# Batch 0's first q and last v in head pairs, W1's second quarter in halves, and a new order of the opening

## The chip, the cores and the metric

The kernel runs on one core of one Trainium2 chip. The metric is the device time of one execution in microseconds. Before the change the median of three runs was 257.46 us (256.84 to 258.04).

The core has five engines with queues of their own, each worked through in order: TensorE (PE, with its weight loads shown as PEld), VectorE (DVE), ScalarE (ACT), GpSimd (POOL) and SyncE (SP, which here only issues DMAs). An instruction that waits holds up all that stands behind it on its engine. Tiles lie in SBUF; matmuls write to PSUM, which has eight banks.

## What is computed

Linear attention on 8 batches, 8 heads, 576 positions and 64 columns a head, and a two-layer network over all 4608 tokens:

```python
q_s = softmax(q, axis=-1)          # over the 64 columns of a head
k_s = softmax(k, axis=2)           # over the 576 positions
kv  = einsum('bhsd,bhse->bhde', k_s, v)
x   = einsum('bhsd,bhde->bhse', q_s, kv)   # -> (4608, 512)
h   = x @ w_in                     # 512 x 2048
out = (h * sigmoid(h)) @ w_out     # 2048 x 512
```

Inputs and output are float32.

## The kernel before

The tokens are done in tiles: tile 0 is the whole of batch 0 (576 tokens), then come tiles of 448 and 512 tokens. The attention of a later batch is computed beside the network of an earlier tile. From tile 1 on the network's products are done by a scheme with seven products in place of eight, for which sums and differences of weights (`WS`, `T1` to `T4`) are made once by VectorE.

All instructions are issued from one list of names, `ORDER` (line 18), written out by hand: the order of the names gives the order on each engine and each DMA queue. Only dependencies between tiles set waits beyond it. `op` (line 584) binds each name to a function.

The names that matter for the opening, with `b.c` standing for batch and half of the heads (c = 0 is heads 0 to 3, c = 1 is heads 4 to 7; a half consists of two head pairs):

- `lq`, `lk`, `lv` load a half of q, k or v (`load`, line 146; 576 KB). Batch 0's go through SP's queue, those of batches 1 and 2 through POOL's, later ones through SP's again.
- `eq` is exp of q on ScalarE (line 160), `z` the row sums and reciprocal on VectorE (line 203), `n` the product with it (line 213). `tr` transposes q on TensorE in nine pieces (line 231) and `tc..a`, `tc..b` copy the result out of PSUM, five pieces on ScalarE and four on VectorE (line 240).
- `ek` is exp of k on ScalarE (line 167). `vc` casts v into `vaug` (line 170), which has a column of constants beside each head for the sums over positions.
- `kv` (line 244) multiplies k and v, 36 small matmuls for a half, row block by row block (nine of them); `kc` (line 256) divides by the sums, giving `kvn`.
- `X` multiplies q with `kvn` (line 278) and `x..a`, `x..v` copy the token tile out to `XT` (line 288).
- `heat0` to `heat3` are matmuls on a constant tile whose results nobody reads (line 561).
- `W1a0`, `W1a1`, `W1b`, `W1c`, `W1d` load w_in in four quarters of four blocks of 128 columns (line 565), with a cast to float16 on the way, through POOL's queue. W1a is in two halves of rows already. The name `gate` stands ahead of them: a copy of one element of k0.0 on GpSimd, so that W1's transfers start when that k has landed. `W2a` to `W2d` load w_out (line 571). The transfers of q1, k1 and v1 stand between these in the same queue.
- The wide stage: for each of the 16 blocks fb, `w{fb}.0` and `w{fb}.1` are four matmuls each of 288 columns (line 304, matmul at 307), over rows 0 to 255 and 256 to 511 of w_in; `h{fb}` is a tanh on ScalarE (line 318), `v{fb}` a product on VectorE (line 322). `WIDE` (line 302) gives the PSUM banks, in turn 4, 2, 0 and 6, so w(fb+4) waits for v(fb). `p{fb}` (line 443) is the second layer of the first 512 tokens.
- `WS{g}.{i}` (line 372) are VectorE's sums and differences of w_in: `WS1.1` needs W1b, `WS1.3` W1b and W1d, `WS0.3` W1a and W1c.

Batch 1's attention (`eq1`, `qp1`, `z1`, `n1`, `ek1`, `vc1`, `tr1`, `tc1`, `kv1`, `kc1`, `xt1`, `x1`) is laid between the end of the wide stage and the `p` steps.

Four very small reads, `touch` (line 547), stand at the start of GpSimd's queue; they fetch a few elements of w_in, w_out, k and v of batch 0 into a tile that is overwritten later.

Of the kernel before, what the change touches and what calls it, by code (L numbers as in the profile page):

```python
# [8 lines left out]
FP32 = mybir.dt.float32  # L9
# [12 lines left out]
    w5.0 w5.1 v0 v2 h3 w4.0 w4.1 WS0.1 h5 w6.0 w6.1 v3 h4 W2b2 v4 w7.0 w7.1 v5 w8.0 w8.1 h7 h6 v7 w9.0 w9.1 lv1.0 h8  # L22
    v6 w11.0 w11.1 v8 h9 lv1.1 w10.0 w10.1 eq1.0.0 v9 h11 WS0.2 w12.0 w12.1 eq1.1.0 v11 h10 w13.0 w13.1 WS1.1
    eq1.0.1 v10 h12 w15.0 w15.1 qp1a h13 v12 w14.0 w14.1 eq1.1.1 v13 qp1b WS1.2 W2c1 p0 h14 z1.0 ek1.0 p1 z1.1.0
    n1.0 z1.1.1 p2 h15 ek1.1 v15 p3 WS1.4 W2c2 tr1.0 v14 lq2.0 p4 tc1.0a tc1.0b lq2.1 n1.1 p5 W2d p6 lk2.0 T1 vc1.0
    lk2.1 p7 tr1.1 lv2.0 vc1.1a vc1.1b gcopy WS1.3 kv1 lv2.1 tc1.1b p8 tc1.1a kc1 WS0.3 xt1.0 xt1.1 x1.0a x1.1v p9
    x1.2a x1.3v g1.1.1 xs1.1 xs1.2 xs1.4 g1.1.2 s1.1.0a WS0.4 p10 xs1.3 eq2.0 a1.1.0 p11 eq2.1 z2.0 g1.1.6 g1.1.5
    s1.1.1a z2.1 n2.0 p12 ek2.0 g1.1.7 p13 s1.1.2v n2.1 ek2.1 p14 a1.1.2 g1.1.4 p15 tq2 u1.1.4 g1.1.3 po2v vc2.1
    po1a m0 po3v po0a a1.1.1 u1.1.0 vc2.0 m1 lk3.0 mu0 m2 T2 lq3.0 mu1 lq3.1 m3 u1.1.2 lk3.1 T3 m4 lv3.0 u1.1.1
    lv3.1 m5 T4 mu2 os0 mu4 kv2 mu5 m6 mu3 kc2 X2.0 mu6 X2.1 x2.0v m7 x2.1a x2.3a x2.2v g2.1.1 mu7 xs2.1 xs2.2  # L30
    g2.1.2 s2.1.0v b1.1.0 ek3.0 S1.1 g2.1.6 eq3.1 lk4.0 S1.2 b1.2.0 os1 s2.1.1a b1.1.1 xs2.3 xs2.4 eq3.0 a2.1.0
    g2.1.7 vc3.0 sa1 b1.2.1 lq4.0 z3.1 s2.1.2a g2.1.5 vc3.1 ek3.1 b1.6.0 a2.1.2 n3.1 lk4.1 g2.1.4 z3.0 g2.1.3 u2.1.0
    g2.0.2 u2.1.4 wa1 n3.0 b1.6.1 a2.1.1 u2.1.2 g2.0.1 sb1 S1.3 kv3 tq3 s2.0.0a b1.5.0 kc3 u2.1.1 S1.4 g2.0.6 b1.7.0
    s2.0.1v lv4.0 ek4.1 b1.7.1 lv4.1 a2.0.0 os3 g2.0.7 sc1 ek4.0 b1.5.1 s2.0.2v g2.0.5 eq4.0 lk5.0 wc1 lq4.1 g2.0.4
    a2.0.2 os2 b1.4.0 vc4.0 lk5.1 z4.0 u2.0.4 g2.0.3 u2.0.2 b1.3.0 lv5.0 vc4.1 a2.0.1 u2.0.0 lq5.0 b1.4.1 n4.0 X3.0
    wl1v X3.1 kv4 x3.0a x3.1v x3.2a b1.3.1 kc4 x3.3a xs3.1 u2.0.1 g3.1.1 xs3.2 wb1 g3.1.2 s3.1.0a xs3.3 xs3.4 g3.0.2
    S2.1 g3.1.6 S2.2 eq4.1 b2.2.0 s3.1.1a b2.1.0 z4.1 ek5.0 b2.1.1 a3.1.0 g3.1.7 n4.1 sa2 ek5.1 b2.6.0 s3.1.2v
    g3.1.5 vc5.0 tq4 g3.1.4 a3.1.2 u3.1.0 b2.6.1 u3.1.4 S2.3 g3.1.3 sb2 lq5.1 g3.0.1 u3.1.2 a3.1.1 lv5.1 lk6.0
# [24 lines left out]
    s8.0.2v b7.7.1 a8.0.2 b7.5.1 sc7 u8.0.0 g8.0.4 wc7 g8.0.3 u8.0.4 b7.4.0 a8.0.1 u8.0.2 b7.3.0 u8.0.1 b7.3.1 e1.0
    wb7 S8.1b e1.1 o7.0 S8.1a b7.4.1 S8.2a sa8 S8.2b e2.0 wl7v e6.0 S8.3 o7.1 e6.1 e2.1 sb8 e5.0 waE0 S8.4 qa00g
    qa01s e7.0 waE1 e7.1 qa11g qa10a e5.1 sc8 wcE0 e3.0 wcE1 qc01g wxE0 qc11a e3.1 wbE0 qc00a wxE1 qb00g qb01s e4.0
    wbE1 qc10s qb10g e4.1 qb11s wlE0a ql01a ql00s wlE1a ql11a ql10s
"""


@with_exitstack  # L70
def kernel(
# [9 lines left out]
    nc = tc.nc  # L81
    B, H, S, D = q.shape
# [737 lines left out]
```

## Time and profile before

| what | value |
|---|---|
| median of three runs | 257.46 us (256.84 to 258.04) |
| the profiled execution, whole time | 257.18 us |
| its span in the trace | 255.1 us |
| granted TensorE clock, mean | 0.999 |
| DMA rate over the span, mean | 180 GB/s |
| first matmul of the wide stage (line 307) starts | 15.07 us |
| first matmul of the second layer (line 445) starts | 30.76 us |

Landings of the opening's transfers (start of the issue plus time to landing, from the DMA issues of the trace), in us:

| transfer | issued | landed |
|---|---|---|
| q0.0, q0.1 (SP) | 0.74, 1.27 | 4.34, 6.04 |
| k0.0, v0.0 (SP) | 1.76, 2.27 | 8.39, 9.82 |
| k0.1, v0.1 (SP) | 2.79, 3.33 | 11.32, 12.78 |
| W1a0, W1a1 (POOL) | 8.59, 9.34 | 14.22, 15.51 |
| W1b, W1c, W1d (POOL) | 10.08, 10.83, 11.56 | 18.51, 20.96, 23.57 |
| q1.0, q1.1 (POOL) | 12.29, 13.00 | 25.04, 26.50 |
| W2a (POOL) | 13.73 | 28.93 |
| k1.0, k1.1 (POOL) | 14.80, 16.05 | 30.43, 31.90 |
| W2b1, W2b2 (POOL) | 18.80, 21.25 | 33.00, 34.30 |
| v1.0, v1.1 (POOL) | 23.86, 25.69 | 35.83, 37.29 |

A row of a timeline gives the start, the length, the engine, the line, the operation, what is written and read, and the shape; in brackets stands the idle time of the engine before it and what ended it. SPq and POOL rows named DMA_DIRECT2D are the issues of transfers, not the transfers. Rows with xN are N instructions in a row put together. The chain of waits is followed back from the last instruction of the kernel to what released each one. An engine's busy share is over the whole span.

### The profile page before, as it was taken

The page shows a single profiled execution, that of the slowest core. Times are in us where ns is not written, and L with a number is a line of the kernel's source. Part 1 is how long each engine was busy: PE and PEld are TensorE (multiplying, and loading weights), DVE is VectorE, ACT ScalarE, POOL GpSimd, SP SyncE. Part 2 cuts the span into 40 slices and gives each one's busy share as a digit, 9 for nine tenths or more (in the row PEclk, how much of TensorE's full clock was granted, in tenths as well). Part 3 has the DMA queues.
Part 4 walks back from the last instruction along what each step waited for, and adds up shares of the span by engine and source line. Part 5 has one row for each costly group of instructions (what it writes and reads, how often), then busy time and mean ns, then how long its engine had stood idle before and what let it go on. Part 6 is the DMA issues. An engine that isn't in the chain of part 4 may idle for free.

```text
span 255.1 us, 6464 instructions
## 1 busy us (share of the span) xinstructions
PE 248.8 (98%) x2732; PEld 204.5 (80%) x2732; DVE 205.6 (81%) x276; ACT 190.9 (75%) x225; POOL 67.6 (27%) x66
## 2 busy tenths in 40 slices
PE   8799999999999999999999999999999999999994
PEld 3467746757888888888888888888888888888883
DVE  2958999987999989998998986896569836886752
ACT  4766886898999999999879979737587656664311
POOL 4652592630541531430083050006000000000022
PEclk9999999999999999999999999999999999999999
DMA  6999999879969938996965950030807000700355
GB/s 239 350 197 299 300 301 310 340 175 395 356 119 279 403 114 216 345 296 155 299 241 87 251 195 0 3 67 18 174 4 164 4 0 4 155 12 0 69 139 123
DMA packets 36172, 45.89 MB, mean 180 GB/s; under 512 B 16416, under 2 KB 21216, under 8 KB 36144
## 3 DMA queue, kind: packets, MB, share of 16 engines
q1 hardware_dynamic: 29456, 33.56, 45.5%
q0 software_dynamic: 6288, 11.60, 17.7%
q10 hardware_dynamic: 400, 0.33, 0.6%
q8 instruction: 21, 0.34, 0.5%
q14 instruction: 7, 0.06, 0.1%
HBM read 36.70 MB, written 9.44 MB: 181 GB/s over the span
## 4 chain that ended last, share of the span: by engine, by line
PE 91%; DMA 5%; ACT 1%; SPq 1%; DVE 0%; issue 0%; ACTq 0%
PE PS L503 37%; PE PS L425 36%; PE PS L307 6%; PE PS L445 5%; DMA vt<-in_v_dram 4%; PE PS L335 2%; PE PS L282 2%; PE PS L248 2%; SPq L152 1%; DMA out_dram<-ow 1%; PE PS L234 0%; DVE ow L754 0%; ACT ow L767 0%; ACT vaug L142 0%; ACT sc L739 0%; ACT XT L142 0%
## 5 line engine op out<-in xcount | busy, mean ns | idle before, releaser
L403 DVE TENSOR_TENSOR h<-PS,h 128x1024 f32<-128x1024 f32 (+1 forms) x45 | 54.1, 1205 | 8.9 <-PE PS L425 7.9
L503 PEld LDWEIGHTS <-GT 128*128 128x128 f16 x512 | 50.1, 98 | 5.9
L425 PEld LDWEIGHTS <-WS 128*128 128x128 f16 x480 | 46.6, 98 | 6.7 <-issue 0.8
L409 ACT ACTIVATE GT<-h 128x1024 f16<-128x1024 f32 (+1 forms) x45 | 46.8, 1049 | 1.1 <-DVE h L403 1.0
L503 PE MATMUL PS<-W,GT 128*128 128x256 f16 x384 | 47.3, 273 | 0.0
L425 PE MATMUL PS<-XS,WS 128*128 128x256 f16 (+1 forms) x360 | 45.0, 272 | 0.0
L142 ACT COPY h<-PS 128x1024 f32<-128x1024 f32 (+1 forms) x31 | 31.1, 1004 | 17.1 <-PE PS L425 16.0
L503 PEld LDWEIGHTS <-S 128*128 128x128 f16 x384 | 37.1, 98 | 4.6
L425 PEld LDWEIGHTS <-W 128*128 128x128 f16 x360 | 35.2, 98 | 4.4
L216 POOL TENSOR_TENSOR eq<-eq,rzq 128x1152 bf16<-128x1152 bf16 x13 | 27.4, 2117 | 37.5 <-DVE rzq L211 36.6
L503 PE MATMUL PS<-T,S 128*128 128x256 f16 x256 | 32.2, 273 | 0.0
L144 POOL CAST vaug<-vt 128x1152 bf16<-128x1152 f32 x12 | 15.8, 1332 | 60.5 <-DMA vt<-in_v_dram 60.1
L425 PE MATMUL PS<-XT,W 128*128 128x256 f16 (+1 forms) x240 | 29.7, 272 | 0.0
L144 DVE COPY h<-PS 128x1024 f32<-128x1024 f32 (+1 forms) x14 | 17.0, 1213 | 8.8 <-PE PS L425 3.9
L772 POOL DMA_DIRECT2D out_dram<-ow x5 | 2.7, 547 | 70.0 <-DVE ow L754 70.0
L163 ACT ACTIVATE eq<-qt 128x1152 bf16<-128x1152 f32 (+1 forms) x18 | 18.8, 1055 | 2.9 <-DMA qt<-in_q_dram 2.7
L168 ACT ACTIVATE ek<-kt 128x1152 bf16<-128x1152 f32 x16 | 18.6, 1163 | 1.7 <-DMA kt<-in_k_dram 1.5
L207 DVE TENSOR_REDUCE zq<-eq 128x18 f32<-128x1152 bf16 x14 | 18.8, 1343 | 1.3 <-ACT eq L163 1.2
L409 ACT ACTIVATE GT<-PS 128x1024 f16<-128x1024 f32 (+1 forms) x15 | 15.2, 1013 | 6.1 <-PE PS L425 6.1
L503 PE MATMUL PS<-T,GT 128*128 128x256 f16 x128 | 16.3, 273 | 0.0
L503 PE MATMUL PS<-W,S 128*128 128x256 f16 x128 | 16.1, 273 | 0.0
L307 PE MATMUL PS<-XT,W 128*128 128x288 f16 x128 | 15.9, 286 | 0.0
(89 smaller groups left out, 334.1 us busy)
## 6 DMA issues: line engine op xcount, KB each, us to landing
out_dram<-ow SPq DMA_DIRECT2D x64, 128.0 KB, 2.9
qt<-in_q_dram SPq DMA_DIRECT2D x11, 576.0 KB, 6.2
kt<-in_k_dram SPq DMA_DIRECT2D x11, 576.0 KB, 7.1
vt<-in_v_dram SPq DMA_DIRECT2D x11, 576.0 KB, 6.5
qt<-in_q_dram POOLq DMA_DIRECT2D x4, 576.0 KB, 9.9
kt<-in_k_dram POOLq DMA_DIRECT2D x4, 576.0 KB, 13.2
vt<-in_v_dram POOLq DMA_DIRECT2D x4, 576.0 KB, 11.8
W<-in_moe_w_in_dram POOLq DMA_DIRECT2D x3, 512.0 KB, 10.1
```

The lines of the kernel that those rows point to most:

```text
L142: eng.copy(out=o, in_=i)
L144: eng.tensor_copy(o, i)
L163: nc.scalar.activation(out=half(st[b]["eq"], cc)[:, :, g0:g1], in_=jgd(b, "qt", cc)[:, :, g0:g1], func=ACT.Exp)
L168: nc.scalar.activation(out=half(ek, cc), in_=jgd(b, "kt", cc), func=ACT.Exp)
L207: nc.vector.reduce_sum(out=z, in_=e, axis=AX.X)
L216: eng.tensor_tensor(out=e, in0=e, in1=r[:, :, :, None].to_broadcast([128, J, 2, D]), op=ALU.mult)
L307: nc.tensor.matmul(out=PS[:, WIDE[fb] + n, 0:S // 2], lhsT=W1[:, c, fb * 128:(fb + 1) * 128], rhs=XTS[0][:, c, n * (S // 2):(n + 1) * (S / ...
L403: nc.vector.tensor_tensor(out=four(t, i), in0=group_bank(t, g), in1=four(t, i), op=ALU.add)
L409: nc.scalar.activation(out=group_out(t, f, n), in_=x, func=ACT.Silu, scale=1.0 / XS)
L425: nc.tensor.matmul(out=PS[:, bank + p // 2, (p % 2) * HT:(p % 2) * HT + width(t)], lhsT=a[:, c, p * 128:(p + 1) * 128], rhs=bb[:, c, 0:wid ...
L445: nc.tensor.matmul(out=PS[:, 2 + tb, :], lhsT=GTS[t % 2][:, fc, tb * 128:(tb + 1) * 128], rhs=W2[:, fc, :], start=(fc == 0), stop=(fc == N ...
L503: nc.tensor.matmul(out=PS[:, bank, m * HN:(m + 1) * HN], lhsT=a[:, fc, m * 128:(m + 1) * 128], rhs=bb[:, fc, :], start=(first and fc == 0) ...
```

## The change

Batch 0's first q (`lq0.0`) and last v (`lv0.1`) are loaded in two transfers each, one for each head pair. The exp and the row sums of q0.0 are done a head pair at a time. The cast of the second head pair of the last v is split: rows 0 to 4 on VectorE (`vc0.1b`), rows 5 to 8 on ScalarE (`vc0.1c`, new). W1's second quarter, `W1b`, is loaded in two halves of rows (`W1b0`, `W1b1`).

The order is new from the first name up to batch 1's x: `tr0.0` and `tc0.0a` stand ahead of `ek0.0`, `tr0.1` ahead of `kv0.0`, `tc0.1b` ahead of `kc0.0`, `heat1` ahead of `tr0.0`, and `heat3` ahead of `X0.0`; the order of the wide stage's blocks, of batch 1's loads against W2's and of the WS steps differs. Behind `x1` the list is as before.

Batch 7's first k and v are loaded whole, as the load in two parts is kept for its first q only. The small reads go through a helper that now takes an engine; all four are given GpSimd, as before.

```diff
-    lq0.0 lq0.1 lk0.0 lv0.0 lk0.1 lv0.1 heat0 eq0.0 z0.0 eq0.1 gate W1a0 W1a1 W1b W1c W1d lq1.0 lq1.1 W2a n0.0 z0.1
-    ek0.0 tr0.0 heat1 n0.1 vc0.0 tc0.0a tc0.0b kv0.0 kc0.0 tr0.1 ek0.1 X0.0 heat2 vc0.1a vc0.1b tc0.1a tc0.1b kv0.1
-    kc0.1 heat3 x0.0a x0.0v X0.1 w0.0 x0.1a x0.1v w2.0 lk1.0 w1.0 w1.1 lk1.1 w2.1 h1 w0.1 h2 v1 w3.0 w3.1 h0 W2b1
...
+    lq0.0.0 lq0.0.1 lq0.1 lk0.0 lv0.0 lk0.1 lv0.1.0 lv0.1.1 gate W1a0 W1a1 W1b0 W1b1 W1c W1d heat0 eq0.0.0 eq0.0.1
+    eq0.1 heat1 z0.0.0 z0.0.1 n0.0 tr0.0 z0.1 tc0.0a ek0.0 n0.1 tc0.0b vc0.0 lq1.0 tr0.1 ek0.1 vc0.1a lq1.1 tc0.1b
+    W2a kv0.0 vc0.1c heat3 kc0.0 X0.0 heat2 vc0.1b tc0.1a x0.0a kv0.1 kc0.1 x0.0v X0.1 w0.0 x0.1v w2.0 w1.0 W2b1
+    x0.1a w0.1 h0 WS0.1 w1.1 v0 w3.0 w2.1 h1 v1 w3.1 w4.0 lk1.0 W2b2 w5.0 w5.1 h2 v2 lv1.0 w6.0 h3 v3 h5 w4.1 v5
+    w6.1 lk1.1 lv1.1 WS1.1 W2c1 w7.0 h4 w7.1 h6 h7 v4 w9.0 w9.1 w8.0 w8.1 v6 v7 h9 v9 w11.0 h8 w11.1 WS1.3 WS0.3
+    w10.0 v8 h11 WS1.2 w10.1 w13.0 w13.1 eq1.0.1 h10 eq1.0.0 qp1a v11 w12.0 w12.1 h13 v10 w15.0 qp1b v13 eq1.1.1 h12
...
-    def load(b, name, src, cc, eng, parts=1):
-        t = ld.tile([128, 2, J * D], FP32, name=name)
-        st[b][name, cc] = t
+    def load(b, name, src, cc, eng, g0=0, g1=2):
+        if (name, cc) not in st[b]:
+            st[b][name, cc] = ld.tile([128, 2, J * D], FP32, name=name)
+        t = st[b][name, cc]
...
+        eng.dma_start(out=t[:, g0:g1], in_=x[:, 2 * cc + g0:2 * cc + g1, :])
+
+    def loads(b, name, src, cc, eng, parts):
         for g in range(0, 2, 2 // parts):
-            h = slice(g, g + 2 // parts)
-            eng.dma_start(out=t[:, h], in_=x[:, 2 * cc:2 * cc + 2, :][:, h, :])
+            load(b, name, src, cc, eng, g, g + 2 // parts)
...
-    def vcast(b, cc, eng, g0=0, g1=2):
-        o = vaug[:, :, 2 * cc + g0:2 * cc + g1, 0:D]
-        i = jgd(b, "vt", cc)[:, :, g0:g1, :]
+    def vcast(b, cc, eng, g0=0, g1=2, j0=0, j1=J):
+        o = vaug[:, j0:j1, 2 * cc + g0:2 * cc + g1, 0:D]
+        i = jgd(b, "vt", cc)[:, j0:j1, g0:g1, :]
...
-    touch(0, w_in[0:510])
...
+    for i, x in enumerate((w_in[0:510], w_out[0:2046], k[0].rearrange("h s d -> (h s) d"), v[0].rearrange("h s d -> (h s) d"))):
+        touch(i, x, nc.gpsimd)
...
+            if (x, c) in (("q", 0), ("v", 1)):
+                for g in range(2):
+                    op(f"l{x}0.{c}.{g}", load, 0, x + "t", src, c, nc.sync, g, g + 1)
+            else:
+                op(f"l{x}0.{c}", load, 0, x + "t", src, c, nc.sync)
+        if c == 0:
+            for g in range(2):
+                op(f"eq0.0.{g}", exp_q, 0, 0, g, g + 1)
+                op(f"z0.0.{g}", qsum, 0, 0, g)
...
-    op("vc0.1b", vcast, 0, 1, nc.vector, 1, 2)
+    op("vc0.1b", vcast, 0, 1, nc.vector, 1, 2, 0, 5)
+    op("vc0.1c", vcast, 0, 1, nc.scalar, 1, 2, 5, J)
...
-("W1b", 4, 4, 0, 4), 
+("W1b0", 4, 4, 0, 2), ("W1b1", 4, 4, 2, 4), 
...
-                op(f"l{x}{b}.{c}", load, b, x + "t", src, c, dma, 2 if b == 7 and c == 0 else 1)
+                op(f"l{x}{b}.{c}", loads, b, x + "t", src, c, dma, 2 if (x, b, c) == ("q", 7, 0) else 1)
```

More of the change, by code (lines that the diff above doesn't have):

```diff
@@ L24 @@
[L24 to L38, printed above, removed]
@@ L618 @@
     op("gate", lambda: nc.gpsimd.tensor_copy(gate, st[0]["kt", 0][0:1, 1, 0:1]))
[L619 removed]
+    for x, f, n, c0, c1 in (("W1a0", 0, 4, 0, 2), ("W1a1", 0, 4, 2, 4), ("W1b0", 4, 4, 0, 2), ("W1b1", 4, 4, 2, 4), ("W1c", 8, 4, 0, 4), ("W1d", 12, 4, 0, 4)):
         op(x, load_w1, f, f + n, c0, c1)
```

87 lines of the change are left out of this document (48 added, 39 removed).

## Prediction

> **What bounds the kernel now.** I read the page's busy times first, then the chain of waits in order of time, then the timeline of the first 16 us, then the DMA issues one by one. Busy times, and the shares of the chain by engine:
>
> ```profile
> PE 248.8 (98%) x2732; PEld 204.5 (80%) x2732; DVE 205.6 (81%) x276; ACT 190.9 (75%) x225; POOL 67.6 (27%) x66
> ...
> PE 91%; DMA 5%; ACT 1%; SPq 1%; DVE 0%; issue 0%; ACTq 0%
> ```
>
> TensorE is the bound, and the 5% of DMA has to be found in time. The chain in order of time (start, length, what) has it in one piece:
>
> ```profile
> 3.33 9.45 DMA vt<-in_v_dram
> ...
> 12.81 0.67 ACT vaug L142
> 13.48 0.59 ACT qT L142
> 14.07 0.60 ACT XT L142
> ...
> 14.70 0.44 PE PS L282 x8
> 15.14 15.79 PE PS L307 x128
> 30.92 3.45 PE PS L445 x16
> ```
>
> The last of batch 0's loads (lv0.1) is issued at 3.33 and lands 9.45 later, at 12.78. Until then nothing can be done about it; from 15.07 on TensorE has work without a gap (windows of 1 us over the wide stage are busy 1.00 each, and the waits of PE after 12 us are empty) until its tail at 250 us. So the kernel's time is (start of the first wide matmul) + 240 us, unless an edit tears a hole into the rest. What lies between the landing and that start is read from the timeline (start, length, engine, line, what):
>
> ```profile
> 10.21 1.36 DVE L216 TENSOR_TENSOR eq<-eq,rzq 128x1152 bf16<-128x1152 bf16 x1
> 11.06 0.48 PE L248 MATMUL PS<-vaug,ek 64*64 64x65 bf16 x36 [0.21 <-ACT vaug L142]
> 11.49 1.17 ACT L168 ACTIVATE ek<-kt 128x1152 bf16<-128x1152 f32 x1
> 12.73 0.82 PE L563 MATMUL PS<-XS 128*128 128x512 f16 x3
> 12.81 0.67 ACT L142 CAST vaug<-vt 128x576 bf16<-128x576 f32 x1 [0.15 <-DMA vt<-in_v_dram]
> 12.81 0.76 DVE L144 CAST vaug<-vt 128x576 bf16<-128x576 f32 x1 [0.51 <-DMA vt<-in_v_dram]
> 13.53 0.56 PE L248 MATMUL PS<-vaug,ek 64*64 64x65 bf16 x36
> 14.35 0.29 DVE L261 TENSOR_TENSOR kvn<-PS,rz 128x128 bf16<-128x128 f32 x1
> 15.07 1.15 PE L307 MATMUL PS<-XT,W 128*128 128x288 f16 x8
> ```
>
> Both casts of the last v start 0.03 after the landing and take 0.67 and 0.76; kv0.1 follows at 13.53, ends at 14.09; its normalisation and X0.1 take the 0.98 up to 15.07. The window 2 to 11 us has the DMA engines busy 0.95 to 1.05, so 12.78 itself is set by bytes, and no bytes are added or taken away.
>
> **The change part by part.** Durations are from this execution (span 255.1, 257.18 with what lies around it; the median of the runs is 257.46, so 0.28 above it).
>
> *Casts of the last v.* lv0.1 comes in two head pairs. k0.1 landed at 11.32 and v0.1 at 12.78, so the first half should land about half way, at 12.05 (bounds: 11.32 and 12.78). ScalarE takes exp of k0.1 at 11.35 instead of 11.49, because tc0.0a, which stood ahead of it at 10.91, now runs before ek0.0; it ends at 12.52, and vc0.1a (0.67) runs from about 12.45 to 13.1. The other half is now shared: 5 of 9 rows on VectorE, 4 of 9 on ScalarE. ScalarE's casts of 1152 and 576 columns took 1.16 and 0.67, so 0.85 ns a column and 0.18 fixed, and 256 columns are 0.40: 13.0 to 13.4. VectorE's 320 columns lie between its 0.42 for 512 bf16 columns out of PSUM (11.48) and its 0.76 for 576 of this cast; scaled like ScalarE's they are 0.50: 12.81 to 13.31. kv0.1 goes over the rows in order, 4 products each; rows 5 to 8 come 0.28 after the first, so the late piece is no wait. It can start at 13.33 and take the 0.48 of kv0.0 (its own 0.56 had a wait for VectorE's cast in it), so it ends at 13.81 against 14.09: **0.28 won**.
>
> *The first q in halves.* This decides whether TensorE is free by then, as tr0.1 now stands ahead of kv0.0. Halves are 0.73 to 0.85 apart (576 KB land 1.46 to 1.70 apart), so the first lands near 3.6 (bounds 3.5 and 4.34). Exp halves 0.68: 3.6 to 4.3 and 4.36 to 5.04. Half sums of 0.71 (L209 took 1.35 for two): the second ends at 5.79. Reciprocal 0.27, n0.0 1.36: 7.47, against 8.61. z0.1, reciprocal and n0.1 behind it (1.35, 0.27, 1.36): 10.43 against 11.57. tr0.1 is then through at 11.0, kv0.0 runs at 11.05 (its v, cast at 9.85, was ready at 11.01 as before), kvn at 12.05, X0.0 12.1 to 12.45, heat2's three matmuls (0.22 each) to 13.1. That is before 13.33. On ScalarE tc0.0a waits for tr0.0 until 7.95 and ends at 8.65; ek0.0 behind it starts 0.13 later than before and still ends before v0.0 lands at 9.82. If the first half came no earlier than the whole did, 4.34, the same sums give n0.1 at 11.0, kv0.0 11.55, X0.0 12.65, heat2 to 13.7, kv0.1 ending at 14.2: 0.1 **lost**. Bounds of the opening: 0.45 won (VectorE's piece at 0.42, and kvn and X without their 0.1 of waits) to 0.1 lost. I take 0.26 won, 0.28 less 0.02 for the semaphore of the third cast: first wide matmul at **14.81**. ScalarE's x0.0a, which it needs, ran from 13.97 to 14.67 and keeps that place, so it is no limit yet.
>
> *Two more issues on SP* (0.49 each): the last v half is issued at 4.8, for bytes that move near 12. Nothing.
>
> *The wide stage.* 128 matmuls in 15.79 are 0.4935 for each half step w. New turns are 14.81 + 0.4935 x place. W1b's halves: lands were 14.22, 15.51 (W1a), 18.51 (W1b), 20.96, 23.57. w4.0 (place 8, 18.76) needs W1b0, about 17.0; w5.1 (place 10, 19.75) needs W1b1, 18.51: cover 1.2. Before, w5.0 had its turn at 19.02: cover 0.5. W1c is needed at 22.7, W1d by WS1.3 on VectorE at 25.5: covers 1.7 and 1.9. VectorE now does WS1.3, WS0.3 and WS1.2 (0.61 apart) ahead of v8 and v11. Laid end to end from v9 (ends 25.2): v8 to 27.1, v11 to 28.55; w12.0 (bank of w8) has its turn at 27.6, w15.0 (bank of w11) at 28.63. Cover 0.5 and 0.1; semaphore gaps of 0.03 to 0.07 can eat the second, so 0 to 0.2 of stall. I take 0.03.
>
> *POOL's queue.* One more W1 issue (0.75): W1d is issued at 12.3 and its bytes move from 20.96. The reordered W2b, k1 and v1 are the same bytes, so v1.1 still lands at 37.29, W2c1 at 38.40; k1.1 lands at 35.8 instead of 31.90, its exp (1.16) is done at 37.2, ahead of v1.1. kv1's turn moves from 38.87 to 38.6; ScalarE's v1.1 cast ends at 37.99, VectorE's, behind T1 and tc1.0b, at 38.7 as it did at 38.87 before. kv1 takes heads 0 and 1 first, so cover is some 0.1 to 0.3. VectorE has two WS steps fewer there (1.3), so p8, the x copies and g1.1 keep their distance.
>
> *No effect:* the small reads. The diff gives them an engine argument and still passes GpSimd for all four, in the same place. k7.0 and v7.0 load whole again: their exp and cast are single instructions that read both halves anyway.
>
> Sum: 257.18 - 0.26 + 0.03 = 256.95 on the profile's footing, 257.2 beside the median.
>
> **Rivals.** A run-to-run change under 0.5% (1.29 us) can't be told from none here (the three runs span 1.2).
>
> *Nothing won:* the q half lands late, or a heat block or semaphore gap fills the 0.28. For it: kv0.1 has only 0.2 of room behind heat2. Against: VectorE's chain is freed by 1.1. First wide matmul at 15.0 to 15.17, time **257.5**.
>
> *Slower: the stream of transfers slips.* Every load to 52 us queues behind the one before, so a slip of s by W1's split is carried to all. The smallest cover behind it is kv1's 0.1, so the end moves by s - 0.1 - 0.23: slower than before from s = 0.33, by 0.5% from 1.6. For it: halves are more transfers. Against: W1a's halves landed 1.29 apart, twice that is 2.58, whole quarters were 2.45 to 3.00 apart, so s lies between -0.42 and +0.13. Were the split to cost the landing gap of one more half, 1.29, the time would be 257.46 + 1.29 - 0.33 = **258.4**. [...]
>
> *More won:* the 0.45 bound, **257.0**; TensorE can't start before landing plus casts, so nothing beyond.
>
> **How the numbers follow.** Forecast 0.6, nothing won 0.25, slip 0.1 (over 0.5% in 0.06), more won 0.05. Predicted 257.2. Range 256.4 to 258.2: the bounds 257.0 and 257.5, a slip to 0.9, and 0.6 for the scatter of runs. Faster by over 0.5% would need a start at 13.5, before the last cast can end, so only scatter, 0.05; slower 0.08; within 0.5% 0.87.
>
> **What would show it.** First L307 matmul (new line L311) at 14.7 to 14.9; kv0.1 starting by 13.4; n0.0 ended by 7.6; no PE wait in 15 to 31; w15 not waiting on VectorE; v1.1 landed by 37.4. Wrong if the wide stage starts at 15.1 or later, or if W1b1 lands past 19.7.

## Result, and the profile after

| kernel | median of its executions, us | ratio to before (95% interval) |
|---|---|---|
| before | 257.15 (256.84 to 258.04, 6) | |
| changed | 259.16 (258.73 to 259.58, 5) | 1.0071 (1.0050 to 1.0092) |
| changed, run again (e1) | 260.03 (259.37 to 260.76, 4) | 1.0120 (1.0094 to 1.0146) |

The change makes the kernel slower by 2.0 to 2.6 us, where a gain of 0.26 was forecast. One more execution of the changed kernel took 437.29 us at a granted clock of 0.559 throughout; the profile below is therefore that of e1, the same kernel in an execution of 259.37 us.

The page of e1: busy times, the granted clock in 40 slices, and the chain's shares by engine.

```profile
PE 249.8 (97%) x2732; PEld 205.0 (80%) x2732; DVE 204.7 (79%) x277; ACT 191.2 (74%) x227; POOL 66.7 (26%) x67
...
PEclk9979999999999999999999999999999999999999
...
PE 92%; DMA 3%; DVE 2%; ACT 1%; SPq 0%; issue 0%; ACTq 0%
```

The third slice, 12.9 to 19.3 us, has a 7 where before every slice had a 9. The chain of waits in order of time (start, length, what) has another transfer as its first long piece than before: not the last v but the second q, lq0.1, which is now the third transfer of SP's queue.

```profile
1.67 6.21 DMA qt<-in_q_dram
17.86 15.79 PE PS L311 x128
33.64 3.45 PE PS L449 x16
```

The wide stage is as long as it was, 15.79, and the span ends 239.8 after its first matmul (257.6 less 17.79), against 240.03 before (255.1 less 15.07). All of the loss is ahead of the wide stage, which starts at 17.79 instead of 15.07: 1.12 of these 2.72 us are the later landing of the last v, and 1.60 lie between that landing and the first wide matmul. The timeline of e1 from 7 us on:

```profile
7.90 1.16 ACT L167 ACTIVATE eq<-qt 128x1152 bf16<-128x1152 f32 x1 [2.74 <-DMA qt<-in_q_dram]
9.10 1.35 DVE L211 TENSOR_REDUCE zq<-eq 128x18 f32<-128x1152 bf16 x1 [1.46 <-ACT eq L167]
9.29 0.67 PE L238 MATMUL PS<-ident,eq 128*128 128x128 bf16 x9
10.79 1.36 DVE L220 TENSOR_TENSOR eq<-eq,rzq 128x1152 bf16<-128x1152 bf16 x1
12.20 0.82 PE L238 MATMUL PS<-ident,eq 128*128 128x128 bf16 x9 [2.25 <-DVE eq L220]
12.96 0.71 PE L252 MATMUL PS<-vaug,ek 64*64 64x65 bf16 x36
13.60 1.03 PE L565 MATMUL PS<-XS 128*128 128x512 f16 x2
14.13 0.48 DVE L145 CAST vaug<-vt 128x320 bf16<-128x320 f32 x1
14.56 0.69 PE L286 MATMUL PS<-qT,kvn 64*64 64x320 bf16 x8
15.19 1.21 PE L565 MATMUL PS<-XS 128*128 128x512 f16 x3
16.32 0.48 PE L252 MATMUL PS<-vaug,ek 64*64 64x65 bf16 x36
17.42 0.44 PE L286 MATMUL PS<-qT,kvn 64*64 64x320 bf16 x8 [0.61 <-DVE kvn L265]
17.79 0.91 PE L311 MATMUL PS<-XT,W 128*128 128x288 f16 x6
```

Three things stand in it. First, q0.1 landed at 7.88 (6.04 before), so exp, row sums and n0.1 end at 12.15, and tr0.1, which the new order puts ahead of kv0.0, waits 2.25 for it; the last v landed at 13.90 instead of 12.78. Secondly, the casts of that v are done at 14.61, yet kv0.1 starts at 16.32, behind tr0.1, kv0.0, heat3, X0.0 and heat2. Thirdly, the same instructions are slower than before: heat2's three matmuls take 1.21 instead of 0.82, X0.0 0.69 instead of 0.44. The windows of e1 show why (PEclk is the granted clock, DMA share the mean busy share of the 16 DMA engines):

```profile
core 0: us, PE busy (x) PEld busy (x) DVE busy (x) ACT busy (x) POOL busy (x), PEclk, DMA share, GB/s
12.00:13.00 1.00, 0.80 (x13) 0.61 (x17) 0.48 (x2) 1.00 (x2) 1.00 (x2) 0.79 1.13 246
13.00:14.00 1.00, 1.00 (x39) 0.66 (x38) 0.67 (x3) 1.00 (x2) 1.00 (x2) 0.50 1.12 173
14.00:16.00 2.00, 2.00 (x12) 0.47 (x11) 0.61 (x2) 1.78 (x4) 2.00 (x4) 0.50 1.15 171
16.00:18.00 2.00, 1.39 (x48) 0.70 (x47) 1.08 (x4) 0.20 (x1) 1.09 (x2) 1.00 1.14 150
```

At half clock for 0.42 + 1 + 2 = 3.42 us: the granted clock fell just as TensorE got its work. The experiments take these apart: the stream, the clock, and what the rest of the change is worth.

### The profile page after: what moved, and what is told of

The parts are those of the page before. It is cut to its first block, busy times and chain, and to the rows that moved or that the text cites. A ratio compares the mean times of both kernels' runs of the same rounds, so it can differ in the third digit from the quotient of the medians.

```text
span 435.5 us, 6471 instructions
## 1 busy us (share of the span) xinstructions
PE 428.4 (98%) x2732; PEld 274.4 (63%) x2732; DVE 208.3 (48%) x277; ACT 194.6 (45%) x227; POOL 66.2 (15%) x67
## 4 chain that ended last, share of the span: by engine, by line
PE 98%; ACT 1%; DVE 0%; issue 0%
PE PS L507 40%; PE PS L429 37%; PE PS L311 6%; PE PS L449 6%; PE PS L565 3%; PE PS L339 2%; PE PS L252 2%; PE PS L286 2%; PE PS L238 1%; ACT ek L172 0%; ACT vaug L143 0%; ACT qT L143 0%; ACT ow L779 0%; DVE kvn L265 0%; DVE XS L557 0%
## 5 line engine op out<-in xcount | busy, mean ns | idle before, releaser
L507 PEld LDWEIGHTS <-GT 128*128 128x128 f16 x512 | 67.5, 132 | 30.9
L429 PEld LDWEIGHTS <-WS 128*128 128x128 f16 x480 | 62.7, 131 | 30.7 <-issue 2.3
L507 PE MATMUL PS<-W,GT 128*128 128x256 f16 x384 | 80.5, 390 | 0.0
L429 PE MATMUL PS<-XS,WS 128*128 128x256 f16 (+1 forms) x360 | 76.0, 387 | 0.0
L429 PEld LDWEIGHTS <-W 128*128 128x128 f16 x360 | 47.3, 131 | 22.1 <-issue 1.3
L507 PE MATMUL PS<-T,S 128*128 128x256 f16 x256 | 54.1, 389 | 0.0
L429 PE MATMUL PS<-XT,W 128*128 128x256 f16 (+1 forms) x240 | 50.3, 386 | 0.0
L449 PE MATMUL PS<-W,GT 128*128 128x512 f16 x64 | 26.2, 576 | 0.0
L429 PE MATMUL PS<-XS,W 128*128 128x256 f16 (+1 forms) x120 | 25.9, 390 | 0.0
L145 POOL CAST vaug<-vt 128x1152 bf16<-128x1152 f32 x12 | 13.7, 1156 | 77.5 <-DMA vt<-in_v_dram 62.2
L429 PE MATMUL PS<-XT,WS 128*128 128x256 f16 (+1 forms) x120 | 25.4, 385 | 0.0
L311 PEld LDWEIGHTS <-W 128*128 128x128 f16 x128 | 16.7, 131 | 11.4 <-issue 0.4
```

What stands on the lines that cost most here:

```text
L145: eng.tensor_copy(o, i)
L311: nc.tensor.matmul(out=PS[:, WIDE[fb] + n, 0:S // 2], lhsT=W1[:, c, fb * 128:(fb + 1) * 128], rhs=XTS[0][:, c, n * (S // 2):(n + 1) * (S / ...
L429: nc.tensor.matmul(out=PS[:, bank + p // 2, (p % 2) * HT:(p % 2) * HT + width(t)], lhsT=a[:, c, p * 128:(p + 1) * 128], rhs=bb[:, c, 0:wid ...
L449: nc.tensor.matmul(out=PS[:, 2 + tb, :], lhsT=GTS[t % 2][:, fc, tb * 128:(tb + 1) * 128], rhs=W2[:, fc, :], start=(fc == 0), stop=(fc == N ...
L507: nc.tensor.matmul(out=PS[:, bank, m * HN:(m + 1) * HN], lhsT=a[:, fc, m * 128:(m + 1) * 128], rhs=bb[:, fc, :], start=(first and fc == 0) ...
```

## The experiments

Each kernel has 4 to 12 timed executions, one of them profiled, against the kernel before on the same chip (medians 257.15 to 257.41). The ratios and their intervals are those on record; they are not quotients of the medians in the table (e1's would be 1.0102). "v to w" is the time from the last v's landing to the first wide matmul in the profiled execution.

| run | what runs | median, us | ratio (95%) | last v landed | first wide matmul | v to w |
|---|---|---|---|---|---|---|
| | before | 257.15 | | 12.78 | 15.07 | 2.29 |
| e1 | changed | 260.03 | 1.0120 (1.0094–1.0146) | 13.90 | 17.79 | 3.89 |
| e2 | changed, q0.0 whole | 257.69 | 1.0036 (1.0007–1.0065) | 13.09 | 17.92 | 4.83 |
| e3 | changed, v0.1 whole | 259.90 | 1.0120 (1.0099–1.0140) | 13.48 | 18.13 | 4.65 |
| e4 | changed, no small reads | 260.74 | 1.0139 (1.0092–1.0186) | 13.88 | 18.88 | 5.00 |
| e5 | before, q0.0 in two | 259.10 | 1.0078 (1.0049–1.0108) | 14.24 | 16.53 | 2.29 |
| e6 | before, heat1 early | 257.22 | 0.9997 (0.9968–1.0025) | 12.94 | 15.22 | 2.28 |
| e7 | changed, q0.0 whole, heat1 back | 257.42 | 0.9990 (0.9968–1.0013) | 12.98 | 15.40 | 2.42 |
| e8 | changed, heat1 back | 259.63 | 1.0078 (1.0048–1.0107) | 13.91 | 17.89 | 3.98 |
| e9 | before, q0.1 in two | 258.47 | 1.0046 (1.0028–1.0065) | 13.20 | 15.49 | 2.29 |
| e10 | changed, q0.0 and v0.1 whole, heat1 back | 257.42 | 1.0016 (1.0000–1.0033) | 13.13 | 15.66 | 2.53 |
| e11 | before, v0.1 in two | 257.86 | 1.0027 (1.0008–1.0045) | 12.64 | 14.97 | 2.33 |
| e12 | before, W1's gate later | 258.45 | 1.0055 (1.0036–1.0075) | 13.16 | 15.45 | 2.29 |
| e13 | before, small read first on SP | 258.20 | 1.0038 (1.0022–1.0055) | 13.36 | 15.64 | 2.28 |
| e14 | before, q0.0 over two queues | 257.52 | 1.0018 (1.0000–1.0036) | 12.79 | 15.08 | 2.29 |
| e15 | as e10, q0.0 over two queues | 257.16 | 0.9998 (0.9986–1.0010) | 12.99 | 15.36 | 2.37 |
| e16 | as e15, without heat2 | 257.18 | 1.0001 (0.9985–1.0017) | 13.05 | 15.39 | 2.34 |
| e17 | before, without heat2 | 257.32 | 1.0006 (0.9991–1.0021) | 13.00 | 15.28 | 2.28 |
| e18 | as e16, v0.1 in two | 256.60 | 0.9979 (0.9959–0.9998) | 12.70 | 14.72 | 2.02 |

### Which part of the change loses: e1 to e5

e1 is the changed kernel itself. e2 takes one part of it back, the first q's two transfers (lines of `ORDER` are shown here and below only in the part that differs):

```diff
-    lq0.0.0 lq0.0.1 lq0.1
+    lq0.0 lq0.1
...
-            if (x, c) in (("q", 0), ("v", 1)):
+            if (x, c) == ("v", 1):
```

e3 does the same for the last v (`lv0.1` for `lv0.1.0 lv0.1.1`). e4 leaves out the four small reads, whose values nothing uses. e5 adds the first q's two transfers, and nothing else of the change, to the kernel before:

```diff
-            op(f"l{x}0.{c}", load, 0, x + "t", src, c, nc.sync)
+            op(f"l{x}0.{c}", load, 0, x + "t", src, c, nc.sync, 2 if (x, c) == ("q", 0) else 1)
```

> The changed kernel itself once more, for a profile at full TensorE clock. Theory (the loads): the last v piece lands at 14.2 to 14.3 us again, 1.5 later than before, although its bytes are the same, and the first wide matmul starts 1.5 later, at 16.3 to 16.6; time 258.7 to 259.3. Rival (the clock or a wait in the wide stage or behind it): the last v piece lands by 12.9 and the wide stage starts at 14.8 to 15.1, and the loss of some 1.8 us shows as PE idle time between 15 and 60 us or as a granted clock below 1.

> The changed kernel with q0.0 loaded in one transfer; its exp and sums stay in halves. Theory A (the short first transfers let the small reads of GpSimd's queue in at 3.5 us instead of 5.0, and the stream of loads runs at two thirds until 6.5): last v piece lands at 12.7 to 12.9 again, first wide matmul at 15.0 to 15.2 (q is late, so 0.1 lost by the sum of the prediction), time 257.2 to 257.5. Theory B (SP's queue takes no more than six or so transfers at a time: the seventh issue took 1.50 us): seven are left, so about half of the loss stays, landing 13.3 to 13.8, time 257.8 to 258.4. Theory C (the cast, the order or the clock): 258.7 or more.

> The changed kernel with v0.1 loaded in one transfer; its three casts stay. Theory A: q0.0's halves are still first, so v0.1 still lands at 14.0 to 14.4 and the time is 258.9 to 259.5. Theory B: as with q0.0 whole, half of the loss, landing 13.3 to 13.8, time 257.8 to 258.4. Theory C: 258.7 or more, with the last v landed by 12.9.

> The changed kernel without the four small reads (their values are used nowhere). Theory A: nothing cuts into the stream, so the last v piece lands by 12.3 and the first wide matmul starts by 14.6, time 256.5 to 257.1. A rival to that: the small reads only pay early for what the first real transfer from each input would pay; then the landings of k0.0, v0.0 and W1a0 come late instead and the time stays at 258.5 to 259.5. Theory B: the seventh issue still takes 1.5 us and the landing stays at 14 or so, time 258.7 to 259.3.

> The kernel before with one edit: q0.0 is loaded in two transfers, its exp stays whole. Theory (a split at the front costs stream time by itself, whatever the order behind it): the third transfer's descriptors come late, q0.1 lands at 7.4 to 8.3 in place of 6.04 and the last v at 13.4 to 14.0 in place of 12.78; clock 0.997 or more, time 257.9 to 258.6. Rival (the landing is late only with the changed order, through GpSimd's queue): last v at 12.7 to 13.0 and time 257.2 to 257.6.

e5 alone loses 0.78%, as much as the whole change in its first runs (0.71%); e2, without it, has q0.1 back at 5.96 and loses 0.36%. e3 and e4 stay where e1 is, so neither the last v's split nor the small reads are the cause. e5 has the order, the casts and the copies of before, and v to w is the 2.29 of before: in the profiled execution, at granted clock 0.999, 1.46 of the 1.78 us by which the span is longer are the landing of the last v, 14.24; the other 0.32 lie behind the start of the wide stage and were not followed up. Two of its ten executions had a clock of 0.993 (260.21 and 260.25). The windows of before and of e5:

```profile
3.00:4.00 1.00, 1.00 (x4) 0.35 (x3) 0.00 (x0) 0.00 (x0) 0.93 (x4) 1.00 1.05 406
4.00:5.00 1.00, 1.00 (x3) 0.30 (x2) 0.32 (x2) 0.64 (x1) 0.13 (x1) 1.00 1.02 389
5.00:6.00 1.00, 1.00 (x5) 0.44 (x4) 0.44 (x1) 0.53 (x1) 0.00 (x0) 1.00 0.96 300
```

```profile
3.00:4.00 1.00, 1.00 (x4) 0.36 (x3) 0.00 (x0) 0.00 (x0) 0.92 (x4) 1.00 0.87 302
4.00:5.00 1.00, 1.00 (x3) 0.30 (x2) 0.31 (x2) 0.50 (x1) 0.13 (x1) 1.00 0.66 233
5.00:6.00 1.00, 1.00 (x4) 0.41 (x3) 0.30 (x1) 0.66 (x1) 0.00 (x0) 1.00 0.80 233
6.00:7.00 1.00, 1.00 (x4) 0.35 (x3) 1.00 (x1) 0.00 (x0) 0.00 (x0) 1.00 0.88 272
```

The next-to-last column is the DMA share. Before it is about 1 from 3 us on; in e5 it falls to 0.66 between 4 and 5 us and is back at 1 only from 7. The two half transfers land at 3.67 and 4.41, the first sooner than the whole one (4.34), the second 0.07 later, but the data of q0.1 behind them do not follow: it lands at 8.26 instead of 6.04. Nothing later makes that up. The missing share from 3 to 7 (0.13 + 0.34 + 0.20 + 0.12 = 0.79, against 0.04 for before's 5 to 6) is work that the DMA engines did not do, and the last v lands 1.46 later, more than that mean loss: the packets of SP's queue thin out over nearly two microseconds in e5 (43 begin in the quarter-microsecond from 11.75, 25 in that from 12.5, 4 in that from 13.5) and over a little more than one in before (43 from 11.0, 23 from 11.5, 1 from 12.25), which would fit sixteen engines that are no longer done together.

### What about the queue: e9, e11, e13, e14

e9 splits the second transfer instead of the first, e11 the last one (as e5, with `("q", 1)` and `("v", 1)` in place of `("q", 0)`). e13 puts one of the small reads at the front of SP's queue, so that q0.1 is the third transfer without any q being split. e14 has q0.0 in two by the edit of e5, with its second half issued by ScalarE, ahead of the exp of a dummy that stood first there:

```diff
-        nc.gpsimd.dma_start(out=touched[:, i, :, None], in_=x.rearrange("(a p) f -> p a f", a=3)[0:16, :, 0:1])
+        (nc.sync if i == 3 else nc.gpsimd).dma_start(out=touched[:, i, :, None], in_=x.rearrange("(a p) f -> p a f", a=3)[0:16, :, 0:1])
```

```diff
-            eng.dma_start(out=t[:, h], in_=x[:, 2 * cc:2 * cc + 2, :][:, h, :])
+            (nc.scalar if (b, name, cc, g) == (0, "qt", 0, 1) else eng).dma_start(out=t[:, h], in_=x[:, 2 * cc:2 * cc + 2, :][:, h, :])
+            if (b, name, cc, g) == (0, "qt", 0, 1):
+                nc.scalar.activation(out=dummy, in_=dummy, func=ACT.Exp)
...
-    nc.scalar.activation(out=dummy, in_=dummy, func=ACT.Exp)
...
```

> The kernel before, with only the second transfer of the queue (q0.1) in two instead of the first (q0.0). Theory A (two short transfers at the very front of the queue run out before the next one's data follow): the third 576 KB arrives as before, the last v lands at 12.8 to 13.1 and the time is 257.2 to 257.6, ratio 0.999 to 1.002. Rival B (any transfer more among the first of the queue, wherever the split is, costs the stream its rate): k0.0 lands 1 us or more later than 8.4, the last v at 13.8 to 14.3, and the time is 258.3 to 259.3, ratio 1.005 to 1.008, as with q0.0 in two.

> The kernel before, with only the last v in two transfers, its casts as before. Theory (a transfer more at the end of the queue costs 0.2 to 0.3 us of landing, since W1's packets, which are already under way, come between): the second half lands at 13.0 to 13.1, the first wide matmul starts at 15.3 to 15.4, the time is 257.4 to 257.8, ratio 1.000 to 1.002. Rival (the stream slows with any eighth issue, as it does with q0.0 in two): last v at 13.8 or later, ratio 1.004 to 1.008.

> The kernel before, with one of the four small reads (that of v) at the front of SP's queue instead of in GpSimd's. Theory C (the third transfer of the queue starts late, and the bytes of the first two have to cover that; q0.1 is now the third, behind 576 KB alone): q0.1 lands 1 us or more later than 6.04, the last v at 13.6 to 14.4, time 258.3 to 259.4, ratio 1.004 to 1.009. Rival D (it is the q in short transfers that the stream suffers from): everything later by the issue's 0.5 at most, last v at 12.8 to 13.3, time 257.2 to 257.7, ratio 1.000 to 1.002.

> The kernel before, with q0.0 in two, the second half issued from ScalarE's queue ahead of its table load. Theory C: k0.0 is the third of SP's queue as before, with the same 1152 KB of q ahead of it over both queues: last v at 12.6 to 13.2, time 257.0 to 257.6, ratio 0.999 to 1.002. Rival D (short transfers): as with both halves on SP, last v at 13.7 or later, ratio 1.005 to 1.010.

e9: the halves of q0.1 land at 5.11 and 7.21. The second of them, the third transfer of the queue, is late, the DMA share is 0.91 and 0.80 from 4 to 6, and the last v lands at 13.20, 0.42 later than before. It fits neither expectation whole: the stream suffers, but a third as much as in e5. e11: no slip; the last half lands at 12.64, and the 0.27% that the kernel loses stands behind the start (its span ends 240.9 after the first wide matmul, before 240.03; TensorE's waits there come to 0.4). e9 too loses more, some 1.3 us by the medians, than its 0.42 at the landing, and its span ends 240.7 after the first wide matmul without a wait of TensorE. These losses behind the start were not followed up.

e13 goes against theory C as it was put: q0.1, third in the queue behind a tiny read and one whole q, lands 1.69 after q0.0, as before (1.71). The kernel loses 0.38%, of which the loads, all 0.3 to 0.6 later, explain about half: the wide stage starts 0.57 later, and the span ends 241.1 after it. e14 goes against rival D: with one half on each queue both land at 4.05 and 4.23, q0.1 at 5.84, the last v at 12.79. The windows of e14 from 3 to 6 have no dip of the depth of e5's:

```profile
3.00:4.00 1.00, 1.00 (x4) 0.36 (x3) 0.00 (x0) 0.00 (x0) 0.93 (x4) 1.00 1.04 392
4.00:5.00 1.00, 1.00 (x3) 0.30 (x2) 0.32 (x2) 0.75 (x1) 0.12 (x1) 1.00 0.99 371
5.00:6.00 1.00, 1.00 (x4) 0.41 (x3) 0.55 (x1) 0.55 (x2) 0.00 (x0) 1.00 0.94 281
```

So it is not short transfers as such (e14, e11), nor the count (e11 has as many), nor a third place in which a tiny read is counted (e13). The landings show what is common to all: the third load in SP's queue, the tiny read left out, lands between 7.2 and 8.9 in every one of these kernels, whether two whole loads lie ahead of it (k0.0 at 8.39 before, 8.92 in e13) or two halves (q0.1 at 8.26 in e5, 7.88 in e1). In before k0.0 already comes 2.35 behind q0.1, where the loads behind it are 1.43 to 1.50 apart. With q0.0 in halves one load of 576 KB less has landed by then, and e5's slip of 1.46 is what such a load takes in this queue. e11's split stands behind the third place, and there is no slip. Why the third load is late stays open. One reading is that the data of a transfer follow only some time after the last but one in its queue has ended, a time that the length of a whole one between (1.46) hides and that of a half (0.73) doesn't; by it e11's last half should be late too, and it isn't. The pattern is shown, the mechanism is not.

### The clock: e2, e6, e7, e8

e2 has the stream back, but v to w is 4.83. Its waits (engine, what it waited for, total, times, longest) and windows:

```profile
PE PS L252 <- ACT vaug L143: 1.0, 1, 1.0
PE PS L238 <- DVE eq L220: 1.0, 1, 1.0
```

```profile
12.00:14.00 2.00, 1.09 (x38) 0.54 (x37) 0.81 (x4) 2.00 (x3) 2.00 (x4) 0.79 1.21 198
14.00:16.00 2.00, 2.00 (x13) 0.47 (x11) 0.40 (x2) 1.97 (x4) 1.67 (x3) 0.50 0.96 126
16.00:18.00 2.00, 1.39 (x47) 0.67 (x46) 0.97 (x3) 0.07 (x1) 0.51 (x1) 0.85 1.18 189
```

Two waits of 1.0 and then half clock for 0.84 + 2.0 + 0.6 = 3.4 us. Of e2's ten executions six had a granted clock of 0.997 or more over the span and took 257.25 to 257.74; four had 0.993 and took 259.06 to 259.81: about 1.9 us for one such stretch. What lets TensorE idle there is heat1: in the new order its seven matmuls come ahead of tr0.0 instead of behind it, where they used to fill the wait for n0.1. e7 puts it back in e2, e8 in the changed kernel, and e6 takes it forward in the kernel before:

```diff
-    eq0.1 heat1 z0.0.0 z0.0.1 n0.0 tr0.0 z0.1
+    eq0.1 z0.0.0 z0.0.1 n0.0 tr0.0 heat1 z0.1
```

> The kernel before with one edit: heat1's seven matmuls stand ahead of tr0.0, as in the change. Theory (the block of 27 runs at half rate for its first 4 us and so ends at 9.1 to 9.8, not at 7.1; tr0.0 waits for it, and from its end to kv0.0 nothing fills TensorE): tr0.0 starts at 9.1 or later in place of 8.66, TensorE stands idle 1 to 2 us before kv0.0, and a part or all of the executions show a granted clock of 0.993 with a stretch of 3.41 us at 0.5, time 258.5 to 259.5 in those, 257.2 to 257.6 in the others. Rival (the clock falls only because the loads are late): all at 0.997 or more and 257.2 to 257.6.

> The changed kernel with q0.0 in one transfer and heat1 behind tr0.0 again; the last v stays in two transfers, W1b in halves, the order else new. Theory: tr0.0 starts at 8.0 to 8.7, no execution shows the clock of 0.993, and only the 0.3 of the late last v piece (13.09) stands against the 0.28 of the split cast: time 257.1 to 257.6. Rival (tr0.1 ahead of kv0.0 leaves the gap that drops the clock): half of the executions at 0.993 and 259.0 to 259.8 as with heat1 in front.

> The changed kernel with one edit: heat1 behind tr0.0 again. Theory: q0.1 lands at 7.5 to 8.3, so n0.1 ends at 11.8 to 12.5 and tr0.1 waits; heat1 ends at 9.2 or before, the idle time to tr0.1 is 2.5 us or more, so the clock falls all the same: 0.993, time 258.7 to 260. Rival (heat1's place alone decides the clock): 0.997 or more and 257.9 to 258.6, the loss of the late landing alone.

e7: none of ten executions below 0.997, against four of ten in e2 (small numbers), 257.42. e6: one of ten below (259.26), no loss otherwise; in that order kv0.0 does not stand behind tr0.1. Its profiled execution kept the full clock although TensorE waited 1.93 us in one piece, ahead of kv0.0, longer than either wait of e2. So the longest wait does not tell whether the clock falls, and which waits bring it stays open. The kernel before never fell below 0.997 in these runs. e8: with the loads late, the place of heat1 no longer saves it; seven of ten executions at 0.993 or less (median 260.18), three at full clock (257.81, 258.39 and 259.80). In the changed kernel itself the two causes can't be parted by their sum: the one of its executions that kept 0.999 took 258.92, no less than the four at 0.993 (258.73 to 259.58).

### What the rest of the change is worth: e10, e12, e15 to e18

e10 is the changed kernel with both batch 0 splits undone and heat1 back; the order, the cast in three pieces and W1b's halves stay. e15 is e10 with q0.0 in two over two queues, as in e14. e12 is a try at an earlier last v: the gate ahead of W1 reads v0.0 instead of k0.0.

```diff
-    op("gate", lambda: nc.gpsimd.tensor_copy(gate, st[0]["kt", 0][0:1, 1, 0:1]))
+    op("gate", lambda: nc.gpsimd.tensor_copy(gate, st[0]["vt", 0][0:1, 1, 0:1]))
```

> The changed kernel with q0.0 and the last v whole and heat1 behind tr0.0; the new order, W1b in halves and the cast in three pieces stay. Theory (the two splits of batch 0's loads are what loses, the rest of the change gains at most 0.2): last v at 12.7 to 12.9, first wide matmul at 14.9 to 15.2, time 256.9 to 257.4, ratio 0.998 to 1.000. Rival (the order itself or W1b's halves lose something that the late loads hid): first wide matmul at 15.3 or later, ratio 1.001 to 1.004.

> The kernel before, with the gate ahead of W1's transfers waiting for v0.0 instead of k0.0, so W1's issues start 1.4 us later (10.0 instead of 8.59). Theory (W1's packets share the DMA engines with the last v from 11.3 on and make it later): the last v lands 0.2 to 0.6 earlier, at 12.2 to 12.6, the wide stage starts at 14.5 to 14.9, and the time is 256.7 to 257.2, ratio 0.997 to 1.000. Rival (W1a then comes too late for the first wide matmuls: 14.22 and 15.51 become 15.2 and 16.5): no gain at the start, a wait of up to 1 us in the first turns, time 257.3 to 258.3, ratio 1.000 to 1.004.

> The changed kernel with the last v whole, heat1 behind tr0.0, and the second half of q0.0 in ScalarE's queue. Theory C (the loss is the stream's alone; q in halves frees VectorE by 1.1 us as forecast): last v at 12.6 to 13.2, n0.1 ended by 10.8, first wide matmul at 14.6 to 15.0, time 256.5 to 257.2, ratio 0.997 to 1.000. Rival (no gain even then, since TensorE's chain behind the last v is what is left): first wide matmul at 15.0 to 15.4, ratio 1.000 to 1.003.

e12 loses: W1a1 lands at 17.87 instead of 15.51 and TensorE waits for it, by its waits

```profile
PE PS L307 <- DMA W<-in_moe_w_in_dram: 0.8, 1, 0.8
```

and the last v, with W1's transfers issued 1.8 later, lands at 13.16 all the same. So nothing here shows W1's packets setting that landing. It scatters by itself: over the twelve profiled executions with q0.0 whole or on two queues, nothing in front of it and q0.1 whole, it lies between 12.64 and 13.16, which is why v to w is the better measure of an order. (e7's and e2's 12.98 and 13.09 were first put down to the split; e11's 12.64 and e18's 12.70 show that it isn't so.)

e10 and e15 show no gain (e10 up to 0.33% of loss), and v to w, 2.53 and 2.37, is longer than before, where the prediction had 14.81 less 12.78, 2.03. TensorE's timeline in e15, and VectorE's cast:

```profile
11.05 0.68 PE L240 MATMUL PS<-ident,eq 128*128 128x128 bf16 x9 [0.68 <-DVE eq L222]
11.66 0.48 PE L254 MATMUL PS<-vaug,ek 64*64 64x65 bf16 x36
12.25 0.59 PE L566 MATMUL PS<-XS 128*128 128x512 f16 x2
12.77 0.44 PE L288 MATMUL PS<-qT,kvn 64*64 64x320 bf16 x8
13.14 0.82 PE L566 MATMUL PS<-XS 128*128 128x512 f16 x3
13.89 0.48 PE L254 MATMUL PS<-vaug,ek 64*64 64x65 bf16 x36
```

```profile
13.01 0.49 DVE L145 CAST vaug<-vt 128x320 bf16<-128x320 f32 x1 [0.31 <-DMA vt<-in_v_dram]
```

The cast ends at 13.50; kv0.1 starts at 13.89 without a wait in brackets, behind heat2. e16 and e17 take heat2 out (three matmuls whose results nobody reads), and e18 has the last v in two besides:

```diff
-    X0.0 heat2 vc0.1b
+    X0.0 vc0.1b
```

> As e15 (changed order, last v whole, second half of q0.0 in ScalarE's queue), without heat2, three matmuls whose results nobody reads. Theory (TensorE's chain held kv0.1 in e15, at 13.89 where VectorE's cast was done at 13.50): kv0.1 starts 0.55 to 0.65 after the last v's landing, the first wide matmul 2.0 to 2.15 after it, time 0.3 less than e15, 256.7 to 257.0, ratio 0.997 to 0.9995. Rival 1 (the casts hold it, or something else that ends as late): landing to first wide matmul stays at 2.35 or more, ratio 0.9985 to 1.001. Rival 2 (TensorE idles and the granted clock falls): a stretch of 3.4 us at half clock in some executions, those 1.8 us longer.

> The kernel before, without heat2 alone. Theory (in the order of before kv0.1 waits for the casts, and heat2 lies in that wait): landing of the last v to first wide matmul stays 2.25 to 2.3, ratio 0.999 to 1.001. Rival (heat2 holds TensorE there too): 2.0 to 2.15, ratio 0.998 to 0.9995. Where TensorE's idle time of 0.8 us lowers the granted clock, some executions are 1.8 us longer.

> The changed kernel with heat1 behind tr0.0, without heat2, and with the second half of q0.0 in ScalarE's queue; the last v is in two again. Theory (the cast step was right, but heat2 stood in front of kv0.1, and with v whole ScalarE's first cast): kv0.1 starts 0.5 to 0.6 after the last half of v has landed, the first wide matmul 2.0 to 2.15 after it; the landing itself is 0 to 0.2 later than with v whole, 12.8 to 13.2; time 256.6 to 257.0, ratio 0.9975 to 0.9995. Rival (the later landing gives it back, or the granted clock falls in some executions): ratio 0.9995 to 1.002.

e17 was as expected: in the order of before heat2 lies in the wait for the casts. e16 was not: v to w stayed at 2.34, and one of its twelve executions had a clock of 0.993 (258.92). Its kv0.1, from TensorE's timeline:

```profile
13.80 0.63 PE L254 MATMUL PS<-vaug,ek 64*64 64x65 bf16 x36 [0.50 <-ACT vaug L143]
```

With the last v whole, ScalarE's cast of its first head pair can't begin before the landing either and takes its 0.67 after it: heat2 only stood in that wait. In e18 that head pair lands 0.71 earlier. ScalarE's, VectorE's and TensorE's rows:

```profile
12.40 0.97 ACT L143 CAST vaug<-vt 128x576 bf16<-128x576 f32 x2
12.72 0.49 DVE L145 CAST vaug<-vt 128x320 bf16<-128x320 f32 x1
13.11 0.63 PE L254 MATMUL PS<-vaug,ek 64*64 64x65 bf16 x36
...
14.72 2.50 PE L313 MATMUL PS<-XT,W 128*128 128x288 f16 x19
```

kv0.1 starts 0.41 after the landing of the last half (12.70), the wide stage 2.02 after it, and the kernel takes 256.60: 0.9979 of before (0.9959 to 0.9998). It is the one version here that beats the kernel before, by 0.6 us, with an interval that ends just short of 1. The profiled spans differ by 0.61: 0.35 lies ahead of the wide stage, 0.09 of that a sooner landing of the last v, which scatters by more, and 0.26 behind its start, where e1, e7, e10, e15 and e16 gain 0.1 to 0.3 as well.

## Why the prediction was wrong

**The stream.** The step that failed is "so 12.78 itself is set by bytes, and no bytes are added or taken away". It was read from a DMA share of about 1 between 2 and 11 us; but a full share in the old order of transfers says nothing of the share when they are cut otherwise. The windows were wide, too: by single microseconds the rate before was 267 GB/s from 2 to 3 and 300 from 5 to 6, against 406 and 389 between. The first q in two was costed at its landings alone, and those were right (3.64 and 4.45 in e1, forecast near 3.6 and 4.34); the transfer behind them was left at 6.04 and came at 7.88, as the third load in the queue. The bounds of the last v's first half, "11.32 and 12.78", excluded a later one; it landed at 13.17, and the second half at 13.90 in place of 12.78. The two more issues were no cost, as forecast, though the seventh on SP took 1.45 in place of 0.49: the last half was issued at 5.20, long before its bytes moved. The rival that a stream slips was named, with a price in the right direction, but for W1's split.

**n0.0 and n0.1.** n0.0 was forecast to end at 7.47; in e1 it ended at 7.64, 0.97 before the 8.61 of before. n0.1, forecast at 10.43, ended at 12.15, being q0.1's. In e15, where q0.0's halves land together at 4.20 and 4.38, the branch that the prediction kept for a first half no earlier than the whole came true step by step: n0.1 11.0 (measured 11.00), kv0.0 11.55 (11.66), X0.0 12.65 (12.77), heat2 to 13.7 (13.96), kv0.1 ending at 14.2 (14.37). heat2 was set at 0.66 for its three matmuls; from its start to that of kv0.1 it took 0.75.

**TensorE free at 7.5.** The forecast lets tr0.0 follow n0.0 at once and its copy start at 7.95. Wrong: tr0.0 ran at 9.29, though n0.0 was ready at 7.64. heat0 and heat1 stand ahead of it, 27 matmuls in place of 20. The prediction set three later heat matmuls at 0.22 each and gave these no time; in the timeline of before the first 20 took 6.47 us, 0.32 each. They start slow: up to 5.0 us their weight loads follow one another every 0.43, behind that nine take 1.82, 0.20 each, though PEclk on the page is 9 throughout. heat1's seven are the ones that had covered TensorE's wait for n0.1 in their old place.

**The clock.** The prediction has no term for it. The page of before has PEclk 9 in all slices, and a gap on TensorE ahead of kv0.0 was priced at its own length. In e2 a fall cost about 1.9 beside it.

**The cast.** The sum was right where it had its conditions: VectorE's 320 columns took 0.48 to 0.49 (0.50), ScalarE's 256 columns no wait in front of kv0.1, and in e18 v to w was 2.02 (2.03). That the two agree so closely is in part luck: kv0.1 started 0.41 after the landing, 0.14 sooner than forecast, and took 0.63 in place of 0.48. What failed is that "kv0.1 has only 0.2 of room behind heat2" was filled in every version that kept heat2. The rival "nothing won" is what e7, e10, e15 show.

**The rest.** The wide stage ran without a wait of TensorE, as forecast, with the same 15.79; behind it the changed order ends 239.8 to 239.9 after its first matmul in e1, e7, e10, e15, e16 and e18, against 240.0 before. W1's split moved the stream by more than the bounds of s, -0.42 to 0.13, in most executions: W1b's second half landed 2.91 (e3) to 4.06 (e2) behind W1a's, 4.02 in e1, where the whole quarter came 2.55 (e13) to 3.55 (e9) behind in the kernels without the split and 3.00 before; the middle values, 3.7 and 3.1, are 0.6 apart. TensorE did not wait for it. In e10 it reached batch 1, whose last v landed at 38.51 (37.29 before), and kv1 ran at 39.35, at once behind its casts and without a gap on TensorE. The small reads had no effect (e4 gained nothing).

## What to carry to other kernels

A DMA share near 1 describes the transfers as they are cut (from 4 to 5 us it was 1.02 before and 0.66 in e5, with the same bytes to move): before the first transfer of a queue is cut up, ask which transfer stands behind it, and look at its landing, not at the first one's; with the second half on a second queue the transfers behind kept their landings, but the halves came no more than 0.3 ahead of the whole (4.05 and 4.23 in e14, 4.20 and 4.38 in e15, 4.34 before). Filler matmuls have a place like any other instruction: moved ahead of real work they can delay it (tr0.0 ran at 9.29 in e1, its input ready at 7.64), and the wait they leave open can cost a stretch of half clock on top of its own length (3.4 us at half clock in e2's profile; its four executions at 0.993 took about 1.9 us more). A step that is right by itself (the split cast) is worth nothing until every other chain to the same instruction is shorter as well; here the gain came with the earlier half of v, the second queue for q and the removal of heat2 together; v in halves without heat2 and with q whole was not run.

## What the runs showed of the hardware

Two half transfers of 288 KB at the front of SP's queue left the DMA engines busy 0.66 of the microsecond from 4 to 5 us (1.02 before) and moved the landing of the queue's last transfer by 1.46 (e5), though the bytes were the same. The third load of that queue, a small read not counted, landed at 7.21 (e9), 7.88 (e1), 8.26 (e5), 8.39 (before) and 8.92 (e13), with 576 to 1152 KB ahead of it.

TensorE went to half clock for 3.42 us after it had been idle for no more than 2.25 us in one piece (e1), and in e2 after two pieces of 1.0; in e5 one wait of 1.5 and in e6 one of 1.9 left the clock at 1.00. In the 3.4 us ahead of the fall, as long as the stretch of half clock itself, TensorE was busy for 1.2 us in e1 and 1.4 in e2. What brings the fall is not shown; the longest wait alone does not, as e6's was longer than either of e2's.
